# Reciprocal of the denominators by ln and exp on ScalarE, four more matmuls of zeros, and a newly searched order of the units

## The chip, the cores and the metric

The kernel runs on one core of a Trainium2 chip. The metric is the device time of one execution in microseconds (us), as the median of several runs; lower is better. The five engines of the core work side by side, each through its own list of instructions in order: PE (TensorE, with its weight loads PEld), DVE (VectorE), ACT (ScalarE), POOL (GpSimd) and SP (SyncE), which issues all the transfers of this kernel. They wait for one another by semaphores.

## The reference

Two independent blocks share one output of 2048 x 1152. Block A is a gated long convolution over the sequence, computed in the reference with a transform of length 4096. Block B is linear attention with 32 heads of width 18.

```python
def _A_ref(q, k, v, shift_k, ssm_k, ssm_D):        # all of S=2048 by D=576
    ...
    kv = k_shift * v                               # k_shift: causal conv of k with 4 taps
    ...
    y = irfft2(rfft2(kv_pad) * rfft2(kf_pad))[:, 0, :S, :]
    y = y + kv * ssm_D[None, None, :]
    return q * y

def _B_ref(x, wqkv, wo):
    ...
    phi = lambda t: jnp.where(t > 0, t + 1, jnp.exp(t)) + 1e-6
    pq, pk = phi(q), phi(k)
    kv = jnp.einsum("bhsd,bhse->bhde", pk, v)
    z = jnp.einsum("bhsd->bhd", pk)
    num = jnp.einsum("bhqd,bhde->bhqe", pq, kv)
    den = jnp.einsum("bhqd,bhd->bhq", pq, z)[..., None] + 1e-6
    o = num / den
    return o.transpose(0, 2, 1, 3).reshape(B, S, D) @ wo
```

## The kernel before, in words

**The units.** The program is cut into some 300 units of work, each a call of a small function, and the string `ORDER` (L32 to L59) lists them in the order in which they are recorded. A unit such as `h1.0.1.0.A/12` has a name, indices, letters for the engines that do its elementwise work (A for ACT, D for DVE, P for POOL, N for leaving a step to the matmuls that follow), and after the slash the slots of PSUM and of the rings in SBUF that its tiles take. The loop at L853 to L858 calls them one after the other; the order of instructions on every engine follows from this list, and no scheduler changes it. A unit that stands late in the list waits on its engine for those ahead of it.

**Block A.** The 576 channels go in five chunks (`ci` 0 to 4). For each chunk, `cv` (L473) makes the 4-tap convolution of k and multiplies it by v, on DVE or POOL, in products of 128 x 2048 (128 x 1024 for the half chunk 4). `h1` and `u1` (`s1`, L523) multiply the filter and that product with a table of sines, 8 matmuls a unit, and copy the PSUM tile to `Ch` or `Cu`; `ht` and `ut` (`tr`, L536) turn them by a DMA transpose; `h2` and `u2` (`s2`, L544) are a second, small transform whose results are copied to `T` and `SU`; `pX`, `pT` (L565 to L569) multiply these on DVE or POOL, and `pS`, `pA` (L570 to L574) add two halves of a product. Where `pS` or `pA` is N, the unit does nothing and each `i1` of that half issues 8 matmuls more. `i1` (L576, copied to `V`) and `i2` (L595, whose result DVE multiplies by q, L604) transform back, and `st` stores. The sines themselves are made at the start: `ix` on DVE makes index tables `mp` and `mc`, `sin` on ACT (L222) turns them into `G`. Filter chunks are turned by matmuls at first (`hT`, L502); `hd` (L500) adds D to one column of the filter before that, and needs `Dcol` from `dc` (L426).

**Block B.** `xd` turns x (matmuls with the identity, or a DMA transpose), `k` (L446), `q` (L455) and `qt` (L464) project and apply phi with one Exp on ACT (L443) and one operation on DVE (L444). `G`, `zs` and `kv` make the head matrices without projecting v; `M` folds them into wo. `den` (L716) makes all denominators by 40 matmuls into a PSUM tile of 128 x 512; DVE adds an epsilon (L732, L734) and takes the reciprocal (L736) into `rden`. Four units `bc` (L738) and one `bt` (L748) spread the reciprocals over the channels by matmuls with `esel`, and DVE multiplies pq by them (L746, L755). The eight row pairs of `o` and `ol` (L757, L785) are the last matmul, copied to `ob` and stored.

**The start.** `wu` (`_warm`, L74) multiplies zeros with zeros, five matmuls of 128 x 512, before any data is there. `Wj` (L380) spreads the taps by five matmuls, whose source row `ls` loads by DMA (L373). `sw` (L225) makes the last sines and then calls an Exp of one column, so that the table of Exp is loaded early; the load shows as ACT_TABLE_LOAD.

Of the kernel before, what the change touches and what calls it, by code (L numbers as in the profile page):

```python
# [12 lines left out]
ACT = mybir.ActivationFunctionType  # L13
ALU = mybir.AluOpType
# [3 lines left out]
D = 576  # L18
# [55 lines left out]
def _warm(tc, psum, K, n):  # L74

    nc = tc.nc
    zero = K.sm[:, 1984:2048].bitcast(BF)
    ps = psum.tile([128, 4, 128], FP32, name="warm_ps")
    for _ in range({'A': 5, 'B': 8, 'C': 7, 'D': 6}[n]):
        nc.tensor.matmul(ps[:], lhsT=zero, rhs=zero.unsqueeze(1).to_broadcast([128, 4, 128]), start=True, stop=True)  # L80
# [144 lines left out]
def _sine16(tc, K):  # L225
    nc = tc.nc
# [17 lines left out]
def kernel(  # L244
# [13 lines left out]
    nc = tc.nc  # L258
# [358 lines left out]
    B = {}  # L617
# [271 lines left out]
```

## Time and profile before

| what | value |
|---|---|
| median of 3 runs | 161.67 us |
| the three runs | 161.38, 161.67, 163.29 us |
| profiled execution, first to last instruction (span) | 159.3 us |
| busy PE / DVE / ACT / POOL in the span | 147.6 / 139.8 / 128.4 / 65.2 us |
| granted TensorE clock | 1.000 |

The profiled execution has no time of its own beside its span; the median of the runs is 2.37 us above the span and the fastest run 2.08 us. In the rows of the profile the first number of a timeline is the start in us after the span's start, the second the stretch in us from the first start to the last end of the merged instructions; then come engine, line, operation, output and inputs with shapes, and the count. A row of a group ends with the total busy us and the mean ns of one. Instructions of one engine overlap a little, so a stretch of several is shorter than their durations added; matmuls overlap a great deal, and how fast they stream is read from the starts of successive rows.

### The profile page before, as it was taken

How to read it: one execution, taken by the hardware profiler on the slowest of the kernel's cores; microseconds unless marked ns; L12 is line 12 of the kernel's file. 1: busy time of each engine (PE TensorE's matmuls, PEld its weight loads, DVE VectorE, ACT ScalarE, POOL GpSimd, SP SyncE). 2: the span in 40 equal slices, each digit the busy share in tenths (PEclk: the TensorE clock that was granted, in tenths of full speed). 3: DMA queues.
4: the chain of work that ended last, by engine and by line, in shares of the span. 5: the costliest groups of instructions: out<-in, count | busy, mean ns of one | idle time of the engine just before them, and what ended most of it. 6: DMA issues, size and time to landing. Idle time of an engine off the chain costs nothing.

```text
span 159.3 us, 4563 instructions
## 1 busy us (share of the span) xinstructions
PE 147.6 (93%) x1966; PEld 92.2 (58%) x1982; DVE 139.8 (88%) x170; ACT 128.4 (81%) x157; POOL 65.2 (41%) x67
## 2 busy tenths in 40 slices
PE   6799999999999999999998999999878999998990
PEld 1498564465734467467466568576445565677550
DVE  7978699899899999999899989998999999998420
ACT  7979996899997999959996956997999685786331
POOL 7407541806510970008100019589997077400000
PEclk9999999999999999999999999999999999999999
DMA  3999999990979999999999999684999999444282
GB/s 105 352 368 294 255 239 305 152 231 3 164 130 228 243 228 240 189 212 312 159 196 272 242 155 212 187 141 90 268 152 184 175 324 204 124 117 136 62 264 100
DMA packets 74171, 31.92 MB, mean 200 GB/s; under 512 B 52074, under 2 KB 73509, under 8 KB 74150
## 3 DMA queue, kind: packets, MB, share of 16 engines
q1 hardware_dynamic: 74150, 31.62, 91.7%
q8 instruction: 15, 0.25, 0.7%
q14 instruction: 6, 0.05, 0.1%
HBM read 14.97 MB, written 4.72 MB: 124 GB/s over the span
## 4 chain that ended last, share of the span: by engine, by line
PE 66%; POOL 12%; DVE 8%; DMA 6%; issue 3%; ACT 3%; SPq 0%; DVEq 0%; ACTq 0%; POOLq 0%
PE k_ps L451 12%; PE q_ps L460 11%; PE g_ps L659 6%; PE o_ps L776 6%; PE s_ps L532 6%; POOL X L567 5%; PE s_ps L555 5%; DMA Cth<-Ch 4%; PE i_ps L589 3%; POOL T L569 3%; PE hT_ps L511 2%; DMA pqT<-in_A_shift_k_dram 2%; PE xT_ps L337 2%; PE i_ps L602 2%; PE qt_ps L468 2%
## 5 line engine op out<-in xcount | busy, mean ns | idle before, releaser
L451 PE MATMUL k_ps<-wqk,xT 128*128 128x512 bf16 (+1 forms) x154 | 21.3, 282 | 0.3
L532 PEld LDWEIGHTS <-G 128*128 128x128 bf16 x320 | 17.4, 98 | 3.7 <-issue 3.4
L299 ACT ACTIVATE Cu<-s_ps 128x1024 bf16<-128x1024 f32 (+1 forms) x18 | 16.9, 978 | 2.1 <-DMA Cth<-Ch 1.4
L460 PE MATMUL q_ps<-xT,wqk 128*128 128x512 bf16 x78 | 18.2, 379 | 0.1
L451 PEld LDWEIGHTS <-xT 128*128 128x128 bf16 x160 | 11.4, 98 | 10.5 <-issue 0.5
L299 ACT ACTIVATE Ch<-s_ps 128x1024 bf16<-128x1024 f32 (+1 forms) x17 | 15.0, 928 | 3.0 <-PE s_ps L532 2.7
L299 ACT ACTIVATE ob<-o_ps 128x576 bf16<-128x576 f32 (+1 forms) x12 | 7.5, 636 | 11.3 <-PE o_ps L768 5.1
L299 ACT ACTIVATE V<-i_ps 128x1024 bf16<-128x1024 f32 x16 | 15.7, 1034 | 1.0 <-PE i_ps L589 1.0
L659 PE MATMUL g_ps<-pk,x_sb 128*128 128x65 bf16 (+1 forms) x124 | 16.3, 283 | 0.2
L299 ACT ACTIVATE T<-s_ps 128x1024 bf16<-128x1024 f32 x16 | 15.7, 1027 | 0.5 <-POOL at L490 0.5
L490 DVE TENSOR_TENSOR at<-at 128x2048 bf16<-128x2048 bf16 (+1 forms) x13 | 14.9, 1143 | 0.7 <-POOL at L489 0.3
L489 DVE TENSOR_TENSOR at<-k,Wj 128x2048 bf16<-128x2048 bf16 (+1 forms) x13 | 14.8, 1136 | 0.4 <-POOL at L490 0.4
L776 PE MATMUL o_ps<-wo_M,pqT 128*128 128x64 bf16 (+1 forms) x108 | 13.8, 283 | 0.5 <-issue 0.5
L444 DVE SCALAR_TENSOR_TENSOR pk<-pk,k_ps 128x576 bf16<-128x576 bf16 x16 | 11.8, 751 | 2.7 <-ACT pk L443 2.6
L299 ACT ACTIVATE SU<-s_ps 128x1024 bf16<-128x1024 f32 x14 | 14.1, 1029 | 0.0
L659 PEld LDWEIGHTS <-x_sb 128*128 128x128 bf16 x128 | 8.4, 97 | 8.7 <-issue 1.1
L460 PEld LDWEIGHTS <-wqk 128*128 128x128 bf16 x80 | 7.5, 98 | 9.1 <-issue 1.1
L443 ACT ACTIVATE pk<-k_ps,neg 128x576 bf16<-128x576 f32 x16 | 11.6, 745 | 1.2 <-PE k_ps L451 0.9
L604 DVE TENSOR_TENSOR q<-i_ps,q 128x1024 bf16<-128x1024 f32 (+1 forms) x10 | 11.0, 1107 | 1.2 <-PE i_ps L603 1.2
L776 PEld LDWEIGHTS <-pqT 128*128 128x128 bf16 x112 | 7.4, 98 | 7.6 <-issue 0.9
L490 POOL TENSOR_TENSOR at<-at 128x2048 bf16<-128x2048 bf16 (+1 forms) x2 | 6.2, 3097 | 12.9 <-DVE at L489 12.9
L532 PE MATMUL s_ps<-v,G 128*128 128x128 bf16 (+1 forms) x160 | 10.5, 214 | 1.0 <-ACT Cu L299 0.4
(161 smaller groups left out, 349.1 us busy)
## 6 DMA issues: line engine op xcount, KB each, us to landing
x_sb<-in_B_x_dram SPq DMA_DIRECT2D x4, 576.0 KB, 4.7
h_sb<-in_A_ssm_k_dram SPq DMA_DIRECT2D x4, 512.0 KB, 5.1
out_dram<-ob SPq DMA_DIRECT2D x7, 288.0 KB, 3.3
k<-in_A_k_dram SPq DMA_DIRECT2D x1, 1280.0 KB
v<-in_A_v_dram SPq DMA_DIRECT2D x1, 1280.0 KB, 8.5
q<-in_A_q_dram SPq DMA_DIRECT2D x1, 1280.0 KB
wqk<-in_B_wqkv_dram SPq DMA_DIRECT2D x2, 576.0 KB, 7.6
k<-in_A_k_dram SPq DMA_DIRECT2D x1, 1024.0 KB
```

Source lines behind the costliest of these rows:

```text
L299: nc.scalar.activation(out=out, in_=in_, func=ACT.Copy)
L443: nc.scalar.activation(out=out_ap, in_=ps_ap, func=ACT.Exp, bias=K.neg1[0:n, :])
L444: nc.vector.scalar_tensor_tensor(out=out_ap, in0=out_ap, scalar=1.0, in1=ps_ap, op0=ALU.min, op1=ALU.max)
L451: nc.tensor.matmul(ps[:, n0:n1], lhsT=xT[r // 4][:, t, rr * 128:(rr + 1) * 128], rhs=wqk[:, t, D + n0:D + n1], start=(t == 0), stop=(t == 4))
L460: nc.tensor.matmul(ps[:, j, :], lhsT=wqk[:, t, 128 * c:128 * c + 128], rhs=xT[g][:, t, :], start=(t == 0), stop=(t == 4))
L489: on[0].tensor_tensor(out=t_, in0=kk[:, 3 - stage:19 - stage], in1=wb(stage), op=ALU.mult)
L490: on[1].tensor_tensor(out=a_, in0=a_, in1=t_, op=ALU.add)
L532: nc.tensor.matmul(ps[:, bi, 0:dc], lhsT=K.G[ri][:, b, :], rhs=xf(b), start=True, stop=True)
L555: nc.tensor.matmul(ps[q:q + 32, z, :], lhsT=K.W0[64 * z:64 * z + 64, x, :], rhs=Ct[64 * z:64 * z + 64, r, :, j, :], start=True, stop=True)
L604: nc.vector.tensor_tensor(out=qs, in0=ps[:, :, 0:dc], in1=qs, op=ALU.mult)
L659: nc.tensor.matmul(ps[:, n0:n1], lhsT=x_sb[:, r, f0:f0 + fn], rhs=pk[:, r, n0:n1], start=(r == 0), stop=(r == 15))
L776: nc.tensor.matmul(pss[i][:, n0:n1], lhsT=pqT[:, c, r * 128:(r + 1) * 128], rhs=B['M'][:, c, n0:n1], start=(c == 0 and not first), stop=(c ...
```

## The change

**The reciprocal.** `b_den` no longer adds and inverts on DVE. ACT takes Ln of the PSUM tile with the epsilon as bias, in place, and then Exp with scale -1 into `rden`. `_sine16` names the table that holds both Ln and Exp for the load that it makes anyway.

**The zeros.** A second unit `wu.2.B` issues four matmuls of zeros more, right after the first five.

**The order.** The whole list `ORDER` is another one: nearly every unit stands at another place, 49 units have other engine letters, and the slots differ. It keeps all other units.

```diff
-io dl ix.0.0/0 hl.0/0 lz sin.1.0 eps ix.1.0/1 id ls ix.0.1 iw ix.1.1 xl.2 sin.0.0 wk wu.1.A/0 lw.2 dc/1 hd.0 Wj.A/230
+io ix.0.1/0 lz lw.2 wu.1.A/0 ls wu.2.B/1 sin.1.1 ix.1.1/1 sin.0.1 xl.2 id Wj.A/230 dl dc/1 ix.0.0 hl.0/0 hd.0 ix.1.0
...
@@ _warm
-    for _ in range({'A': 5, 'B': 8, 'C': 7, 'D': 6}[n]):
+    for _ in range({'A': 5, 'B': 4}[n]):
@@ _sine16
     nc.scalar.activation(out=K.sm[:, 1536:1984], in_=K.wi, func=ACT.Sin, scale=TWO_PI / 16, bias=K.negpi[:])
+    nc.scalar.preload_act_table_set("natural_log_exp_and_others")
     nc.scalar.activation(out=K.warm[:], in_=K.neg1[:], func=ACT.Exp)
@@ b_den
         den = ps[:, 0:512]
-        nc.vector.tensor_scalar(out=den, in0=den, scalar1=ez[:, 0:1], scalar2=None, op0=ALU.add)
-        with nc.allow_low_precision(reason="the reciprocal is used as bf16"):
-            nc.vector.reciprocal(out=B['rden'], in_=den)
+        nc.scalar.activation(out=den, in_=den, func=ACT.Ln, bias=ez[:, 0:1])
+        nc.scalar.activation(out=B['rden'], in_=den, func=ACT.Exp, scale=-1.0)
```

Three places show what the new order does. The first is ACT at the start of the program, from the zeroing of the tap rows (L377) on. Before:

```order
L377 ACTIVATE pqT<-sm 96x1152
L222 ACTIVATE G_103<-mp,negpi 128x1024
L222 ACTIVATE G_132<-mc,negpi 128x1024
L432 ACTIVATE Dcol<-D_ps 128x5
L500 ACTIVATE h_sb<-h_sb,Dcol 128x1
L299 ACTIVATE Wj<-W_ps 128x4x256 x2
L299 ACTIVATE Wj<-W_ps 128x4x64
L222 ACTIVATE G_132<-mc,negpi 128x1024
L222 ACTIVATE G_103<-mp,negpi 128x1024
L500 ACTIVATE h_sb<-h_sb,Dcol 128x1
L299 ACTIVATE Ch<-s_ps 128x2x32x16 x3
```

ACT at the same place in the changed program:

```order
L377 ACTIVATE pqT<-sm 96x1152
L221 ACTIVATE G_112<-mp,negpi 128x1024
L221 ACTIVATE G_117<-mc,negpi 128x1024
L299 ACTIVATE Wj<-W_ps 128x4x256 x2
L299 ACTIVATE Wj<-W_ps 128x4x64
L432 ACTIVATE Dcol<-D_ps 128x5
L500 ACTIVATE h_sb<-h_sb,Dcol 128x1
L221 ACTIVATE G_117<-mc,negpi 128x1024
L500 ACTIVATE h_sb<-h_sb,Dcol 128x1
L299 ACTIVATE xT<-xT_ps 128x512
L221 ACTIVATE G_112<-mp,negpi 128x1024
L299 ACTIVATE Ch<-s_ps 128x2x32x16 x2
```

The copies of the taps (Wj) now stand ahead of Dcol, the last table of sines stands behind a copy of xT that DVE made before, and two copies of Ch instead of three follow. On PE the nine matmuls of zeros are followed at once by those of Wj, then by the turning of x (20 matmuls) and of both filter chunks 0 and 1 (32), before the first 24 matmuls of `h1`.

The second place is DVE around the denominators, from a copy of SU (L301) to the products with the reciprocals (pqT). Before:

```order
L604 TENSOR_TENSOR q<-i_ps,q 128x8x128
L301 CAST Ch<-s_ps 128x2x32x16
L301 CAST SU<-s_ps 128x2x512
L487 TENSOR_TENSOR at<-k,Wj 128x16x64
L489 TENSOR_TENSOR at<-k,Wj 128x16x64
L490 TENSOR_TENSOR at<-at 128x16x64
L732 TENSOR_SCALAR ez<-den_ps 128x1
L734 TENSOR_SCALAR den_ps<-den_ps,ez 128x512
L736 RECIPROCAL wo_M<-den_ps 128x512
L604 TENSOR_TENSOR q<-i_ps,q 128x8x128 x2
L746 SCALAR_TENSOR_TENSOR pqT<-pqT,bc_ps 128x1024 x2
```

DVE at the same place in the changed program:

```order
L301 CAST SU<-s_ps 128x2x512
L301 CAST V<-i_ps 128x8x32x4
L301 CAST wo_M<-m_ps 128x576
L567 TENSOR_TENSOR X<-SU,T 128x2048
L572 TENSOR_TENSOR X<-X 128x2x512
L569 TENSOR_TENSOR T<-SU,T 128x2048
L604 TENSOR_TENSOR q<-i_ps,q 128x8x128
L732 TENSOR_SCALAR ez<-den_ps 128x1
L604 TENSOR_TENSOR q<-i_ps,q 128x8x128
L745 SCALAR_TENSOR_TENSOR pqT<-pqT,bc_ps 128x1024 x2
```

The add and the reciprocal are gone, three operations of the half chunk's convolution and a copy of Ch have left, and the products X and T of chunk 2, an add, and copies of V and of M have come. On ACT the Ln and the Exp stand behind a copy of SU and ahead of four copies of Cu.

The third place is POOL in the second half, behind the copy of the filter's half chunk (hp). Before:

```order
L518 COPY hp<-h_sb 64x2048
L489 TENSOR_TENSOR at<-k,Wj 128x16x64
L490 TENSOR_TENSOR at<-at 128x16x64
L567 TENSOR_TENSOR X<-SU,T 128x2048
L569 TENSOR_TENSOR T<-SU,T 128x2048
L572 TENSOR_TENSOR T<-T 128x2x512
L567 TENSOR_TENSOR X<-SU,T 128x2048
```

POOL at the same place in the changed program, where the first row of the half chunk's convolution stands ahead of that copy:

```order
L487 TENSOR_TENSOR at<-k,Wj 128x16x64
L518 COPY hp<-h_sb 64x2048
L489 TENSOR_TENSOR at<-k,Wj 128x16x64
L490 TENSOR_TENSOR at<-at 128x16x64
L567 TENSOR_TENSOR X<-SU,T 128x2048
L489 TENSOR_TENSOR at<-k,Wj 128x16x64
L490 TENSOR_TENSOR at<-at 128x16x64
L489 TENSOR_TENSOR at<-k,Wj 128x16x64
```

POOL has given its products of chunk 2 and one of chunk 3 to DVE and taken most of the convolution of the half chunk.

49 lines of the change are left out of this document (24 added, 25 removed).

## The prediction

> **What bounds the kernel now.** I read the page first (span, busy shares, slices), then a table by stage, then the two places that the change rewrites.
>
> ```profile
> span 159.3 us, 4563 instructions
> PE 147.6 (93%) x1966; PEld 92.2 (58%) x1982; DVE 139.8 (88%) x170; ACT 128.4 (81%) x157; POOL 65.2 (41%) x67
> GB/s 105 352 368 294 255 239 305 152 231 3 164 130 228 243 228 240 189 212 312 159 196 272 242 155 212 187 141 90 268 152 184 175 324 204 124 117 136 62 264 100
> ```
>
> Three engines are above 80%, so no single one is worth its busy time; the question is which ends last in each stage. The stages are cut at the first matmul of `k` (14.84), at the first product of `i2` on DVE (95.67) and at the last product with a reciprocal (122.31):
>
> ```profile
> core 0: us, PE busy (x) PEld busy (x) DVE busy (x) ACT busy (x) POOL busy (x), PEclk, DMA share, GB/s
> 0.00:14.84 14.84, 12.02 (x120) 9.02 (x120) 12.08 (x27) 12.77 (x18) 6.97 (x31) 1.00 0.89 279
> 14.84:95.67 80.83, 79.69 (x905) 45.95 (x915) 75.31 (x82) 70.81 (x83) 25.41 (x26) 1.00 1.06 209
> 95.67:122.31 26.64, 24.11 (x455) 16.61 (x454) 25.99 (x33) 23.48 (x31) 24.16 (x8) 1.00 0.90 179
> 122.31:140.00 17.69, 17.14 (x284) 10.84 (x282) 16.58 (x19) 12.91 (x17) 8.62 (x4) 1.00 0.91 202
> 140.00:159.30 19.30, 14.66 (x226) 9.82 (x222) 9.86 (x12) 8.47 (x11) 0.00 (x0) 1.00 0.45 132
> ```
>
> From 14.84 to 95.67 PE is busy 79.69 of 80.83 us: it is the bound, and little DVE work saved there would be worth anything. From 95.67 to 122.31 DVE is busy 25.99 of 26.64 us, and PE's 24.11 us overstates it, since its matmuls overlap: DVE is the bound. At the end neither is.
>
> **The start: zeros and another order (-1.1 us).** The PE rows up to the first `k`:
>
> ```profile
> 1.06 2.31 PE L80 MATMUL warm_ps<-sm 128*128 128x512 bf16 x5 [1.06 <-DVE negpi L127]
> 5.15 2.08 PE L387 MATMUL W_ps<-pqT,sm 97*128 97x512 bf16 x5 [1.56 <-DMA pqT<-in_A_shift_k_dram]
> 7.02 1.91 PE L511 MATMUL hT_ps<-ident,h_sb 128*128 128x128 bf16 x16
> 8.73 1.71 PE L337 MATMUL xT_ps<-ident,x_sb 128*128 128x128 bf16 x16
> 10.28 0.39 PE L342 MATMUL xT_ps<-ident,x_sb 128*128 128x128 bf16 x4
> 14.84 6.43 PE L451 MATMUL k_ps<-wqk,xT 128*128 128x512 bf16 x49
> ```
>
> and from the chain of waits a later group of the same width, at full pace:
>
> ```profile
> 21.27 0.89 PE s_ps L532 x16
> ```
>
> The first transposes go at (8.73 - 7.02) / 16 = 107 ns each, the later matmuls at 0.89 / 16 = 56 ns; the column of the granted clock reads 1.00 all the same. The turns of x in between take (10.28 - 8.73) = 1.55 us, 0.16 us less than sixteen at 107 ns, so the rate doubles about three matmuls before 10.28, near 10.1 us. This is 5 us after the matmuls start again at 5.15, behind a gap in which PE had nothing to do; the five zeros before the gap did not bring it about. W_ps (four matmuls of 512 columns and one of 256) takes 7.02 - 5.15 = 1.87 us, 0.42 us for 512 columns; nine zeros at that pace run from 1.06 to about 5.0. They fill the gap, cost nothing (W_ps waits for its taps until 5.15 anyway, and by the shapes the taps' transfer now has one of 144 KB ahead of it instead of one of 512 KB), and keep PE busy without a break from 1.06 on.
>
> If the 5 us of unbroken work are what counts, the rate doubles at 1.06 + 5 = 6.1; if the 9 us since the first matmul count, it stays at 10.1. I take 6.8, nearer to the first, since the row shows a gap that the zeros close. W_ps then still ends at 7.0 at the slow rate, and the turning of x and of two filter chunks (20 + 32 matmuls) takes 52 x 0.056 = 2.9 us instead of up to 5.6. What PE can use of this is set by ACT and DVE, by these rows:
>
> ```profile
> 6.20 2.22 ACT L299 ACTIVATE Wj<-W_ps 128x1024 bf16<-128x1024 f32 x3 [0.18 <-PE W_ps L387]
> 8.29 1.16 ACT L222 ACTIVATE G<-mc,negpi 128x1024 bf16<-128x1024 int16 x1
> 10.37 0.30 ACT L500 ACTIVATE h_sb<-h_sb,Dcol 128x1 bf16<-128x1 bf16 x1
> L299 ACT ACTIVATE xT<-xT_ps 128x512 bf16<-128x512 bf16 x1 | 0.6, 600 | 0.0
> L299 ACT ACTIVATE T<-s_ps 128x1024 bf16<-128x1024 f32 x16 | 15.7, 1027 | 0.5 <-POOL at L490 0.5
> ```
>
> After the change ACT goes Wj to 8.4, Dcol and the first h_sb (0.1 + 0.3) to 8.8, G to 9.9, h_sb to 10.1, xT to 10.7, the last G to 11.8. Only then can the third unit of `h1` run: 8 matmuls to 12.2, their copy with the one ahead to about 13.4, the second copy of xT (0.6) to 14.0, and `k` starts at about 14.2 instead of 14.84, with five units of `h1` behind it instead of four (8 x 0.056 = 0.45 us). Gain 0.64 + 0.45 = 1.1 us. Bounds: with the rate doubling at 4.5, Wj and all behind it come 0.5 us sooner: -1.6. With the rate doubling at 10.1 as now, the turns end some 1.7 us later, DVE copies the second filter chunk until about 13.4, and `k` starts near 15.6: +0.3.
>
> The Trainium skill, page "TensorE: Matmul & The Clock Gate", section "Part 1: The HAM clock gate (the "warmup" mystery)", has the clock double after one busy window of about 3.4 us that runs freely; an estimate from that page puts it between 4.5 and 7.9 us here, where the start would be worth -1.6 to about -0.8. Its Part 4 says that transposes do not count as busy; here the rate doubled after three microseconds of transposes alone, so the trace speaks against that. If it held, only 1.06 to 7.0 would count, and a whole window would fall in it about 7 times in 10; the rest would be the +0.3.
>
> **Sixteen fewer matmuls (-0.5 us).** The list of before has five N among `pS` and `pA`, by the extra matmuls of `i1`; the list of after has 16 matmuls of `i1` fewer. The chain of waits prices them:
>
> ```profile
> 73.56 2.34 PE i_ps L589 x80
> ```
>
> 16 x 2.34 / 80 = 0.47 us of PE's own stream, on the path wherever PE is the bound.
>
> **The denominators and DVE's middle stage (-2.0 us).** DVE before, from the copy of Ch:
>
> ```profile
> 99.34 1.20 DVE L301 CAST Ch<-s_ps 128x1024 bf16<-128x1024 f32 x1
> 101.60 0.86 DVE L487 TENSOR_TENSOR at<-k,Wj 128x1024 bf16<-128x1024 bf16 x1
> 102.38 0.68 DVE L489 TENSOR_TENSOR at<-k,Wj 128x1024 bf16<-128x1024 bf16 x1
> 103.09 0.69 DVE L490 TENSOR_TENSOR at<-at 128x1024 bf16<-128x1024 bf16 x1
> 103.96 0.76 DVE L734 TENSOR_SCALAR den_ps<-den_ps,ez 128x512 f32<-128x512 f32 x1
> 104.76 3.36 DVE L736 RECIPROCAL wo_M<-den_ps 128x512 bf16<-128x512 f32 x1
> 115.42 6.89 DVE L746 SCALAR_TENSOR_TENSOR pqT<-pqT,bc_ps 128x1024 bf16<-128x1024 bf16 x6
> ```
>
> The prices of what comes, and of what ACT pays:
>
> ```profile
> L567 DVE TENSOR_TENSOR X<-SU,T 128x2048 bf16<-128x2048 bf16 x7 | 9.0, 1285 | 0.2 <-ACT SU L299 0.2
> L569 DVE TENSOR_TENSOR T<-SU,T 128x2048 bf16<-128x2048 bf16 x7 | 8.5, 1218 | 0.4 <-POOL X L567 0.4
> L572 DVE TENSOR_TENSOR X<-X 128x1024 bf16<-128x1024 bf16 x4 | 2.7, 684 | 0.0
> L301 DVE CAST V<-i_ps 128x1024 bf16<-128x1024 f32 x2 | 2.4, 1220 | 0.0
> L301 DVE CAST ob<-o_ps 128x576 bf16<-128x576 f32 x4 | 3.0, 751 | 3.9 <-PE o_ps L768 3.9
> L443 ACT ACTIVATE pq<-qt_ps,neg 128x512 bf16<-128x512 f32 x2 | 1.4, 690 | 0.0
> L569 POOL TENSOR_TENSOR T<-SU,T 128x2048 bf16<-128x2048 bf16 x2 | 8.1, 4070 | 5.8 <-DVE X L567 5.7
> ```
>
> Out between the first `i2` and the last `bc` on DVE: 0.76 + 3.36 + (0.86 + 0.68 + 0.69) + 1.20 = 7.55 us. In: X 1.29, its add 0.68, T 1.22, V 1.22, M at ob's 0.75 = 5.16 us. Net -2.4 us. So more than half of the reciprocal's 4.1 us is spent again, on products that POOL made before at 4.07 us each. No row shows Ln, or Exp to this tile; the Exp of 128 x 512 from PSUM takes 0.69 us, so the two cost ACT 1.4 us (at worst two copies of 1024 columns, 2.1 us; never a gain). In the list they stand behind one copy of SU, and PE has 8 + 8 + 16 matmuls' work (i2 and two `u1`, about 1.8 us) between the denominators and the first `bc`: the chain 0.15 + 1.4 us and its handovers fits, just. ACT's load in this stage rises by these 1.4 us and by copies: one of Ch and one of T come (2 x 1.03), one of V and one of M go (1.03 and about 0.7, by the widths), +0.3. That makes 23.48 + 1.7 = 25.2 us against DVE's 25.99 - 2.4 = 23.6: ACT is late next. It would allow 26.64 - 25.2 = 1.4 us, and some more because its copies overlap by about 0.1 us each (two of 1.03 take 1.94 at 145.22, below). I take -2.0, nearer to DVE's -2.4. Bounds: -4.1, if the chain from the denominators to the products alone sets the end; 0, if ACT's new place in the order makes it wait.
>
> **The end (+0.5 us).** From 122.31 on DVE's work falls by some 2.7 us at the same prices, but DVE is idle 9.4 of the last 19.3 us, so I cost that at nothing. The new list puts `i2` of the half chunk right behind the second `i1` of that chunk; before, an `i2` of another chunk stood between, and even so:
>
> ```profile
> 145.22 1.94 ACT L299 ACTIVATE V<-i_ps 128x1024 bf16<-128x1024 f32 x2 [0.80 <-PE i_ps L589]
> PE i_ps L602 <- ACT V L299: 0.6, 1, 0.6
> ```
>
> PE waited 0.6 us for those two copies; without the 0.9 us of cover it waits up to 1.5. Two thirds of it may return, since `o` behind it finds ACT less crowded: +0.5, bounds 0 and +1.
>
> **The sum.** -1.1 - 0.5 - 2.0 + 0.5 = -3.1 us against the profiled span of 159.3: 156.2. The median of the runs stands 2.37 us above that span, so 161.67 - 3.1 = 158.6 us. About 2% (3.2 us) is what a measurement of this kernel tells from no change: the likeliest case lies just inside it.
>
> **The rivals.**
> The whole chain counts. If PE waits in the middle stage only through the reciprocal, the full 4.1 us go and the end costs nothing: -1.1 - 0.5 - 4.1 = -5.7, 156.0 us. For it: the six products at 115.42 run without a gap to 122.31, and `o` waits for them. Against it: DVE got 5.2 us of other work there.
> No help from clock or DVE. The rate still doubles at 10.1 (+0.3), ACT takes all that DVE gives (0), the end costs +1: with the -0.5 that is +0.8, 162.5 us. For it: ACT would stand at 25.2 of 26.6 us.
> A transpose comes late (the other side). The first turn of Ch is needed earlier: the page of before has it at
>
> ```profile
> 14.54 5.75 SPq L539 DMA_TRANSPOSE Cth<-Ch x1
> 31.02 0.56 PE s_ps L555 x16
> ```
>
> 16.5 us ahead of its matmuls. In the new order six `k` (7.4 us by the rows at 14.84), two units of `h1` (0.9) and a `q` (2.2) stand between, so PE wants it at about 24.7, while DVE finishes the last quarter of Ch behind a copy of xT, near 17.4. With 5.75 us it lands at 23.2, 1.5 us early. Some 8 us more would be needed to end over 2% slower than before (1.5 + 3.1 + 3.2): a queue blocked by the loads that stand beside it (1.0 MB of v, 0.6 MB of x at the 239 to 305 GB/s of those slices are 5 to 7 us). Then 165 us or more.
> That the Ln brings a third table load is excluded by the list: it has two, as before.
>
> **How the numbers follow.** Likeliest case (157.4 to 160.2) 0.47, of which a third lies below 158.4, the 2% line; whole chain 0.26; no help 0.18; late transpose 0.09. Faster by over 2%: 0.26 + 0.16 = 0.42. Within 2%: 0.31 + 0.18 = 0.49. Slower: 0.09. The range reaches from the whole chain to no help, 155.8 to 162.6, and leaves out the late transpose (0.09) and about a third of the whole chain's cases, which lie lower (0.09).
>
> **What would show it.** The start is right if the transposes of the changed kernel go at 56 ns from about 7 us and `k` starts near 14.2; wrong if they go at 107 ns to 10. The middle is right if Ln and Exp take 0.6 to 0.8 us each, and the stretch from the first `i2` product to the last `bc` product shrinks from 26.6 to about 24.6 with ACT as busy as DVE; if it shrinks to 22.5 the whole chain counted. The end is right if PE waits 1 to 1.5 us for V behind the last `i1`. A wait of PE for a DMA of Cth near 25 us would show the late transpose.

## The result: slower by 4.0%, and the profile after

| what | before | after |
|---|---|---|
| median of 4 runs each | 161.70 us | 167.94 us |
| the runs | 161.38 to 163.29 us | 166.70 to 168.56 us |
| ratio to before, 95% interval | | 1.0398 [1.0339, 1.0457] |
| span of the profiled execution | 159.3 us | 166.9 us |
| granted TensorE clock, mean | 1.000 | 0.988 |
| busy PE / DVE / ACT / POOL | 147.6 / 139.8 / 128.4 / 65.2 us | 149.2 / 141.7 / 131.6 / 74.0 us |

The forecast was 158.6 us, in a range of 155.8 to 162.6. The kernel is slower, and the range does not hold the time. The ratios, here and below, leave out a kernel's runs that lie over 1.5% above its fastest.

The table by stage of the kernel after, cut at the same three events (first matmul of `k`, first product of `i2` on DVE, last product with a reciprocal); the columns are the stretch, the busy time of PE, PEld, DVE, ACT and POOL, the granted clock, the DMA share and GB/s:

```profile
0.00:14.86 14.86, 12.51 (x132) 8.69 (x133) 12.09 (x25) 12.75 (x18) 6.76 (x30) 1.00 0.85 262
14.86:95.37 80.51, 79.50 (x890) 45.18 (x900) 75.60 (x82) 71.24 (x86) 34.01 (x29) 1.00 1.02 215
95.37:127.73 32.36, 24.58 (x433) 16.70 (x433) 30.02 (x33) 23.55 (x29) 26.93 (x10) 0.95 0.71 135
127.73:166.90 39.17, 32.62 (x513) 20.93 (x512) 23.95 (x28) 24.02 (x31) 6.33 (x3) 0.99 0.66 163
```

Against before the stages are 0.02 us longer, 0.32 shorter, 5.72 longer (32.36 against 26.64) and 2.18 longer (39.17 against 36.99), which makes the 7.6 us of the spans. So three quarters of the loss lie in the middle stage, the one that the prediction expected to gain 2.0 us.

The timeline of DVE there in the kernel after (start, length, engine, line, operation):

```profile
102.89 3.66 DVE L567 TENSOR_TENSOR X<-SU,T 128x2048 bf16<-128x2048 bf16 x1
106.58 2.50 DVE L572 TENSOR_TENSOR X<-X 128x1024 bf16<-128x1024 bf16 x1
109.00 3.13 DVE L569 TENSOR_TENSOR T<-SU,T 128x2048 bf16<-128x2048 bf16 x1
112.06 1.21 DVE L604 TENSOR_TENSOR q<-i_ps,q 128x1024 bf16<-128x1024 f32 x1
113.19 0.14 DVE L732 TENSOR_SCALAR ez<-den_ps 128x1 f32<-128x1 f32 x1
```

and POOL's at the same time:

```profile
101.54 3.92 POOL L518 COPY hp<-h_sb 64x2048 bf16<-64x2048 bf16 x1
105.42 3.11 POOL L489 TENSOR_TENSOR at<-k,Wj 128x1024 bf16<-128x1024 bf16 x1
108.61 2.44 POOL L490 TENSOR_TENSOR at<-at 128x1024 bf16<-128x1024 bf16 x1
111.02 5.04 POOL L567 TENSOR_TENSOR X<-SU,T 128x2048 bf16<-128x2048 bf16 x1
```

Read the two side by side. X, its add and T were priced at 1.29, 0.68 and 1.22 us; they read 3.66, 2.50 and 3.13, 6.1 us more. X is issued at 102.89 while POOL copies until 105.46, and ends 1.1 us after that: nearly its own length. POOL's next product begins at 105.42 and ends at 108.53, 2.0 us after X is done, about the 2.1 us that it takes alone; and so on in turn, each one ending when its own work has followed the end of the other engine's. The product `q` at 112.06 reads PSUM and takes its usual 1.21 us, although POOL is in a product of 5 us.

What waits behind that: `ez` and so the Ln on ACT,

```profile
113.43 0.66 ACT L734 ACTIVATE den_ps<-den_ps,ez 128x512 f32<-128x512 f32 x1 [4.62 <-DVE ez L732]
114.12 0.60 ACT L735 ACTIVATE wo_M<-den_ps 128x512 bf16<-128x512 f32 x1
```

and PE, by its table of waits (engine, tile, line, whom it waited for: total, times, longest):

```profile
PE i_ps L602 <- ACT V L299: 3.5, 2, 2.1
PE s_ps L532 <- DVE q L604: 3.0, 1, 3.0
PE D_ps L430 <- DMA sm<-in_A_ssm_D_dram: 1.2, 1, 1.2
...
PE s_ps L555 <- DMA Cth<-Ch: 0.9, 1, 0.9
```

Ln and Exp take 0.66 and 0.60 us, as forecast. ACT stands idle for 4.6 us before them: PE's last matmuls of the denominators end at 109.33, and DVE comes to `ez` 3.9 us later, at 113.19. PE waits 3.0 us for DVE to free the tile that `q` reads, and 2.1 us in the middle and 1.4 us at the end for ACT's copies of V, where 0.6 us at the end was all before.

### The profile page after: what moved, and what is told of

It reads as the page before. It is cut to its first block, busy times and chain, and to the rows that moved or that the text cites. A ratio compares the mean times of both kernels' runs of the same rounds, so it can differ in the third digit from the quotient of the medians.

```text
span 166.9 us, 4537 instructions
## 1 busy us (share of the span) xinstructions
PE 149.2 (89%) x1953; PEld 91.5 (55%) x1970; DVE 141.7 (85%) x164; ACT 131.6 (79%) x161; POOL 74.0 (44%) x70
## 4 chain that ended last, share of the span: by engine, by line
PE 45%; DVE 23%; DMA 13%; POOL 9%; ACT 5%; issue 2%; SPq 1%; DVEq 0%; POOLq 0%; ACTq 0%
PE g_ps L659 9%; DMA Ctu<-Cu 6%; PE k_ps L451 6%; PE s_ps L532 5%; PE o_ps L775 5%; PE i_ps L589 4%; DMA Cth<-Ch 3%; PE s_ps L555 3%; DMA sm<-in_A_ssm_D_dram 3%; DVE at L490 3%; DVE at L489 3%; POOL at L489 2%; POOL at L490 2%; DVE X L567 2%; PE i_ps L602 2%
## 5 line engine op out<-in xcount | busy, mean ns | idle before, releaser
L451 PE MATMUL k_ps<-wqk,xT 128*128 128x64 bf16 (+1 forms) x155 | 21.1, 283 | 0.3
L489 POOL TENSOR_TENSOR at<-k,Wj 128x1024 bf16<-128x1024 bf16 (+1 forms) x5 | 15.5, 3101 | 7.5 <-issue 7.4
L299 ACT ACTIVATE SU<-s_ps 128x1024 bf16<-128x1024 f32 x16 | 15.8, 1022 | 2.1 <-PE s_ps L555 2.1
L299 ACT ACTIVATE T<-s_ps 128x1024 bf16<-128x1024 f32 x17 | 16.8, 1019 | 0.2 <-PE s_ps L555 0.2
L299 ACT ACTIVATE Cu<-s_ps 128x1024 bf16<-128x1024 f32 (+1 forms) x16 | 15.4, 1000 | 1.4 <-DMA Cth<-Ch 0.9
L299 ACT ACTIVATE Ch<-s_ps 128x1024 bf16<-128x1024 f32 (+1 forms) x16 | 14.2, 918 | 1.9 <-PE s_ps L532 1.9
L572 POOL TENSOR_TENSOR T<-T 128x1024 bf16<-128x1024 bf16 x3 | 6.4, 2125 | 20.8 <-ACT ob L299 14.7
L490 DVE TENSOR_TENSOR at<-at 128x2048 bf16<-128x2048 bf16 (+1 forms) x12 | 14.2, 1179 | 0.8 <-POOL at L489 0.4
L299 ACT ACTIVATE ob<-o_ps 128x576 bf16<-128x576 f32 (+1 forms) x13 | 8.2, 636 | 8.0 <-PE o_ps L767 4.2
L569 DVE TENSOR_TENSOR T<-SU,T 128x2048 bf16<-128x2048 bf16 x9 | 12.9, 1433 | 0.0
```

The costliest lines, as they stand in the source:

```text
L299: nc.scalar.activation(out=out, in_=in_, func=ACT.Copy)
L451: nc.tensor.matmul(ps[:, n0:n1], lhsT=xT[r // 4][:, t, rr * 128:(rr + 1) * 128], rhs=wqk[:, t, D + n0:D + n1], start=(t == 0), stop=(t == 4))
L489: on[0].tensor_tensor(out=t_, in0=kk[:, 3 - stage:19 - stage], in1=wb(stage), op=ALU.mult)
L490: on[1].tensor_tensor(out=a_, in0=a_, in1=t_, op=ALU.add)
L569: e.tensor_tensor(out=t[:], in0=s['SU', hf][:], in1=t[:], op=ALU.mult)
```

## The experiments

Theory 1 after the result: DVE's products from SBUF and POOL's work exclude each other, and the new order puts them side by side ahead of the denominators. Theory 2: PE's waits for V, and the drop of the clock behind its waits, carry the time, and the collision only fills idle time of DVE. Theory 3: the small parts (Ln and Exp, zeros) cost it. The first four kernels take the change apart; all their ratios are to the kernel before on the same chip.

**DVE's three operations moved behind the last reciprocal product (e1).**

```diff
-u2.2.1.1.A/03 pX.2.0.D/0 pA.2.0.D cv.4.0.P pT.2.0.D
+u2.2.1.1.A/03 cv.4.0.P
...
-h1.4.0.1.A/2 bc.1/30 ut.3.1/0
+h1.4.0.1.A/2 bc.1/30 pX.2.0.D/0 pA.2.0.D pT.2.0.D ut.3.1/0
```

> The changed kernel, with X, its add and T of chunk 2 (first half) moved on DVE from ahead of the denominators to behind the last bc product, where POOL's block of work should be nearly over. Nothing is left out. Port theory (a DVE operation with two inputs in SBUF and a POOL operation shut each other out): the stretch from the first i2 product to the last bc product falls from 32.4 us to 23 to 25 us, the three operations take their 1.2, 0.7 and 1.2 us again, ACT no longer waits 4.6 us for ez, and the time is 161 to 163 us. Chain theory (the handovers DVE, ACT, ACT, PE of ln and exp hold PE): the time stays above 166 us, since the chain is the same. Transfer theory (late transposes at the end): 165 us or more, since the end keeps its 39 us.

Measured: 167.61 us, ratio 1.038 [1.0317, 1.0444], the same as the change itself. DVE's part of the timeline in this run:

```profile
106.57 1.23 DVE L604 TENSOR_TENSOR q<-i_ps,q 128x1024 bf16<-128x1024 f32 x1 [4.61 <-PE i_ps L603]
109.83 0.16 DVE L732 TENSOR_SCALAR ez<-den_ps 128x1 f32<-128x1 f32 x1 [2.04 <-PE den_ps L729]
...
123.66 1.22 DVE L567 TENSOR_TENSOR X<-SU,T 128x2048 bf16<-128x2048 bf16 x1
124.92 0.69 DVE L572 TENSOR_TENSOR X<-X 128x1024 bf16<-128x1024 bf16 x1
```

and what PE met there:

```profile
126.80 0.40 PE L589 MATMUL i_ps<-W,T 64*128 64x128 bf16 x4 [2.90 <-DVE T L569]
```

Away from POOL the operations have their old lengths, and the collision is gone. The stretch from the first `i2` product (94.39) to the last product with a reciprocal (which ends at 123.75) is 29.36 us, 3.0 us shorter, where theory 1 had expected 23 to 25; but T is now late for PE by 2.9 us, and the 2.1 us for V stay. The time of 161 to 163 us that theory 1 expected did not come: the run put a wait of the same size elsewhere, so it does not show what the collision costs as a whole.

**Add and reciprocal back on DVE and the named table left out, all else as after the change (e2).**

```diff
-        nc.scalar.activation(out=den, in_=den, func=ACT.Ln, bias=ez[:, 0:1])
-        nc.scalar.activation(out=B['rden'], in_=den, func=ACT.Exp, scale=-1.0)
+        nc.vector.tensor_scalar(out=den, in0=den, scalar1=ez[:, 0:1], scalar2=None, op0=ALU.add)
+        nc.vector.reciprocal(out=B['rden'], in_=den)
```

> The changed kernel, with the add and the reciprocal back on DVE and the table of Exp alone; order and zeros as changed. Port theory: the reciprocal reads PSUM and is not shut out, so it adds its 4.1 us to DVE behind ez less some 1.3 to 2 us of the ACT chain: 169.5 to 171.5 us. Chain theory: without the handovers to ACT 165 us or less.

Measured: 171.23 us, 1.0603 [1.055, 1.0656]. In the new order PE stands right behind the reciprocal:

```profile
116.59 0.39 PE L741 MATMUL bc_ps<-wo_M,esel 32*128 32x512 bf16 x2 [3.27 <-DVE wo_M L735]
```

Against the change itself (167.94) Ln and Exp are worth 3.3 us in the new order. So they are not what made it slower.

**Only Ln and Exp, in the kernel before (e3).** The edit is the one of `b_den` and the named table.

> The kernel before, in its own order, with only the reciprocal by ln and exp. Port theory (the reciprocal is not what went wrong): DVE is the bound from 95.7 to 122.3 us and loses 4.1 us of work while ACT gets 1.3, so 158 to 160.5 us. Chain theory: the chain on ACT is late, 162.5 us or more.

Measured: 161.97 us, 1.0014 [0.998, 1.0049], no change; neither expectation holds the time. The middle stage, cut at the same events as before (first product of `i2`, last product with a reciprocal), and what DVE does with the time it is given:

```profile
95.51:123.22 27.71, 24.29 (x455) 16.69 (x454) 22.02 (x32) 24.70 (x33) 24.48 (x8) 1.00 0.95 180
```

```profile
108.97 1.22 DVE L605 TENSOR_TENSOR q<-i_ps,q 128x1024 bf16<-128x1024 f32 x1 [5.28 <-PE i_ps L604]
```

DVE's load falls from 25.99 to 22.02 us, and DVE simply stands still for 5.28 us until PE delivers the next `i2`. The stage is even 1.07 us longer (27.71 against 26.64). The reason is on ACT, where Ln and Exp (1.3 us) now stand ahead of the copies of V that this `i2` reads. ACT before, and in this run:

```profile
104.75 1.94 ACT L299 ACTIVATE V<-i_ps 128x1024 bf16<-128x1024 f32 x2
...
105.88 1.95 ACT L300 ACTIVATE V<-i_ps 128x1024 bf16<-128x1024 f32 x2
```

PE starts that `i2` at 106.75 before and at 107.88 here, each time right behind the copies. And DVE's second product of `i2` waited for PE already before, soon after the reciprocal, which ended at 108.12:

```profile
109.61 1.23 DVE L604 TENSOR_TENSOR q<-i_ps,q 128x1024 bf16<-128x1024 f32 x1 [0.42 <-PE i_ps L603]
```

DVE was full, and was not the bound.

**Only the four zeros, in the kernel before (e4):** `wu.2.B/1` behind `wu.1.A/0`.

> The kernel before, in its own order, with only the four more matmuls of zeros behind the first five. If unbroken work doubles PE's rate earlier: transposes at 56 ns from about 7 us, the first k at 13.6 to 14.4 us instead of 14.84, and a time of 160.6 to 161.4 us. If the start is held by ACT, DVE and the transfers anyway: the first k at 14.7 to 14.9 us and 161.5 to 161.9 us.

Measured: 160.66 us, 0.9946 [0.9912, 0.998]: 0.9 us faster. PE at the start of this run:

```profile
5.31 1.13 PE L387 MATMUL W_ps<-pqT,sm 97*128 97x512 bf16 x5
6.28 1.15 PE L511 MATMUL hT_ps<-ident,h_sb 128*128 128x128 bf16 x16
7.27 1.06 PE L337 MATMUL xT_ps<-ident,x_sb 128*128 128x128 bf16 x16
...
13.61 2.56 PE L451 MATMUL k_ps<-wqk,xT 128*128 128x512 bf16 x17
```

W_ps ends 0.97 us after its start (6.28 - 5.31) where it took 1.87, and sixteen transposes take (7.27 - 6.28) = 0.99 us, 62 ns each: the rate has doubled at 5.31 already in this execution, and `k` starts at 13.61 instead of 14.84.

**Both small parts in the kernel before (e5).**

> The kernel before in its own order, with both small parts of the change: Ln and Exp on ACT, and four more matmuls of zeros. The ln and exp alone left the time as it was and the zeros alone gained 0.9 us. If DVE's stage is covered by PE (theory now), the two add up to the zeros alone: 160.4 to 161.0. If the earlier start had made DVE the bound of the middle stage, so that the freed 4.1 us count now: 158.5 to 160.0. The new order is the only part that is left out, so a time below the kernel before puts all of the loss on the order.

Measured: 160.36 us, 0.9926 [0.9886, 0.9966]. The two add up to the zeros alone, as far as the intervals tell. This is the fastest version of the study, 0.7% below the kernel before; what is left out of it is the new order, so the loss is in the order.

**The exclusion by itself (m1).** The kernel leaves the whole computation out and writes zeros; it runs products of 2048 columns on DVE and POOL, alone and side by side.

> Leaves the whole computation out (it writes zeros) and only runs DVE and GpSimd operations of this kernel's shapes, first alone, then side by side. Theory 1 (the two engines exclude one another whenever DVE reads two operands from SBUF, for the whole of an instruction): the 2048-wide product takes 1.2 us on DVE and 4.1 us on POOL alone; side by side the two alternate, so that a DVE product reads 4 to 5 us while POOL works and POOL's reads 5.3, and the sum of both lists is the time. Beside a DVE product that reads PSUM both keep their times (1.2 us per 1024 columns, 4.1 us). A DVE copy of 2048 from SBUF to SBUF could go either way. Rival (the long products in the trace of the changed kernel come from something else, such as a shared bank or the transfers): DVE 1.2 to 1.5 and POOL 4.1 to 4.5 in every pairing.

Its timeline (start, stretch, operation, count). Alone, then DVE's products from SBUF, DVE's products of 1024 columns from PSUM, and DVE's copies within SBUF, each beside six products of POOL:

```profile
18.43 7.52 DVE L37 TENSOR_TENSOR dc<-da,db 128x2048 bf16<-128x2048 bf16 x6
...
26.96 16.41 POOL L49 TENSOR_TENSOR pc<-pa,pb 128x2048 bf16<-128x2048 bf16 x4
...
43.61 37.57 DVE L37 TENSOR_TENSOR dc<-da,db 128x2048 bf16<-128x2048 bf16 x12
...
44.84 28.97 POOL L49 TENSOR_TENSOR pc<-pa,pb 128x2048 bf16<-128x2048 bf16 x6
...
81.74 15.06 DVE L41 TENSOR_TENSOR dc<-pq,da 128x1024 bf16<-128x1024 f32 x12
...
82.04 24.70 POOL L49 TENSOR_TENSOR pc<-pa,pb 128x2048 bf16<-128x2048 bf16 x6
...
106.97 31.18 DVE L45 COPY dc<-da 128x2048 bf16<-128x2048 bf16 x12
...
107.66 26.30 POOL L49 TENSOR_TENSOR pc<-pa,pb 128x2048 bf16<-128x2048 bf16 x6
```

Alone a product takes 7.52 / 6 = 1.25 us on DVE and 16.41 / 4 = 4.10 on POOL. Both lists one after the other would be 12 x 1.25 + 6 x 4.10 = 39.6 us; side by side they take 37.57. So 2.0 us of 39.6 overlap. Products that read PSUM keep 15.06 / 12 = 1.25 us and leave POOL at 24.70 / 6 = 4.12. What one DVE operation takes while POOL works, from the groups within POOL's stretch (count, then busy and mean ns), for products and for copies within SBUF:

```profile
L37 DVE TENSOR_TENSOR dc<-da,db 128x2048 bf16<-128x2048 bf16 x6 | 29.8, 4974 | 0.2
...
L45 DVE COPY dc<-da 128x2048 bf16<-128x2048 bf16 x6 | 26.6, 4441 | 0.2
```

A product takes 5.0 us instead of 1.25. A copy is shut out likewise: 4.4 us, where the last five, after POOL is done, take 0.69 each. POOL's copies beside DVE's products, a fourth pairing, stretch them too (12 products in 24.60 us instead of 15.0). Theory 1's mechanism holds, and the rival to it falls.

**POOL out of the way (e6).** In the changed kernel, the conv of the half chunk goes to DVE for its first two steps, and POOL's copy `hp` is made earlier; DVE's X, add and T stay where they are.

```diff
-pA.1.0.P M.2.D/1 ... pA.2.0.D cv.4.0.P pT.2.0.D i1.1.0.0.A/0 ... u1.3.0.1.A/02 hT.4.p/01 ... cv.4.1.PP
+pA.1.0.P hT.4.p/01 M.2.D/1 ... pA.2.0.D pT.2.0.D cv.4.0.D i1.1.0.0.A/0 ... u1.3.0.1.A/02 ... cv.4.1.DD
```

> The changed kernel with POOL out of the way of DVE's products of chunk 2: the first two steps of the half chunk's convolution (three products of 1024 columns) go to DVE, and POOL's copy of the filter's half chunk is done earlier. DVE keeps X, the add and T where they are. Theory 1 (the collision of DVE and POOL on SBUF costs the time): X, the add and T take 1.3 to 1.8, 0.7 and 1.2 us, ez runs near 109.5 instead of 113.2, PE's wait of 3.0 us for q is gone, and the stretch from the first i2 product to the last bc product is 28 to 29.5 us instead of 32.4; the time falls by 3 to 4 us, to 163.5 to 165. Theory 2 (PE's waits for the copies V and the clock that falls behind them cost it, and the collision only fills DVE's idle time): the times of X and T fall, PE still waits 3.5 us for V, and the time stays at 166.5 to 168.

Measured: 164.81 us, 1.0189 [1.0127, 1.0251]. The same operations on DVE:

```profile
101.92 1.65 DVE L567 TENSOR_TENSOR X<-SU,T 128x2048 bf16<-128x2048 bf16 x1
103.61 0.69 DVE L572 TENSOR_TENSOR X<-X 128x1024 bf16<-128x1024 bf16 x1
104.22 1.22 DVE L569 TENSOR_TENSOR T<-SU,T 128x2048 bf16<-128x2048 bf16 x1
...
123.42 3.12 DVE L569 TENSOR_TENSOR T<-SU,T 128x2048 bf16<-128x2048 bf16 x1
```

and the middle stage, up to the last product with a reciprocal:

```profile
94.44:123.51 29.07, 24.30 (x421) 15.81 (x421) 26.24 (x36) 23.34 (x29) 16.52 (x7) 0.96 0.78 154
```

DVE has three more operations, the stage is 3.3 us shorter (29.07 against 32.36), and the time falls by 3.1 us. Theory 1 is right as to the largest part: half of the loss. (X keeps 0.36 us of the collision, the end of `hp`. A new collision came with the edit: T of the second half, at 123.42, takes 3.12 us where it took 1.22 after the change, since POOL's part of the half chunk now stands beside it. The same holds in e7 and e15.)

**And cover for V (e7).** As e6, with `u2.2.1.0` and `den` ahead of the first `i2` of chunk 1.

```diff
-i1.1.0.1.A/1 i2.1.0/2 u2.2.1.0.A/3 den/0 i2.1.1/1
+i1.1.0.1.A/1 u2.2.1.0.A/3 den/0 i2.1.0/2 i2.1.1/1
```

> As the run with POOL out of the way, and PE's u2 unit and the matmuls of the denominators stand ahead of the first i2 of chunk 1, so that PE has 2 us of work while ACT copies V. Theory 1: the collision was nearly all, so this brings at most 1 us more than the run with POOL out of the way alone. Theory 2: PE's wait for V at this place falls from 2.1 to under 1 us, the clock stays near 1.0 in the stage, the stage takes 26.5 to 27.5 us, and the time is 161 to 163.5, at least 1.5 us below the run without the cover.

Measured: 163.95 us, 1.0143 [1.0071, 1.0215]: 0.9 us less than e6, which ran beside it. PE's wait of 2.1 us became 0.5. The gain is inside theory 1's number (at most 1 us) and short of theory 2's (at least 1.5); the clock did not stay up:

```profile
119.21 0.41 PE L555 MATMUL s_ps<-Cth,W 64*32 64x512 bf16 x8 [1.21 <-DVE pqT L745]
...
121.00:122.00 1.00, 0.95 (x20) 0.34 (x16) 1.00 (x2) 0.90 (x3) 1.00 (x1) 0.57 1.13 216
122.00:123.00 1.00, 1.00 (x24) 0.76 (x18) 1.00 (x2) 1.00 (x2) 0.92 (x2) 0.50 1.18 214
123.00:124.00 1.00, 1.00 (x24) 1.00 (x21) 1.00 (x1) 0.89 (x1) 1.00 (x1) 0.50 0.75 150
124.00:125.00 1.00, 1.00 (x21) 0.78 (x16) 1.00 (x1) 0.11 (x1) 0.61 (x1) 0.72 1.19 123
```

The first row is PE's wait of 1.2 us, which ended at 119.21. In the other rows, of 1 us each, the granted clock is halved for about 3.4 us, some 2 us after that wait.

**A failed edit: the half chunk's convolution behind `bc` (e8), and two more on top of it.** `cv.4.1.DD` goes behind `bc.1`, and the copy of T at `h2.3.0.0` to ACT.

> As the run with cover for V, and the two products of the half chunk's convolution that stood between DVE's products with the reciprocals go behind them, and the copy of T there goes to ACT. Theory now (the rest of the middle stage's loss is PE waiting for DVE to free a PSUM tile of bc, 1.2 us, and a drop of the granted clock to 0.66 for 5 us that follows): the last bc product ends near 120 instead of 122.7, PE's wait of 1.2 us for pqT goes, and if the clock stays at 1.00 too, the time falls by 1 to 2.5 us to 161.5 to 163; if the clock drops all the same, by 0.5 to 1. Rival (POOL, now late with the half chunk, or the DMA transposes are what the end waits for): same time as before this edit, 163.7 to 164.2, with the wait moved to Cu or Cth of the half chunk.

Measured: 172.01 us, 1.0721 [1.0676, 1.0767]. Its PE meets the rival:

```profile
133.02 1.04 PE L532 MATMUL s_ps<-v,G 128*128 128x64 bf16 x16 [7.34 <-DVE v L493]
```

The chain of the half chunk's convolution over DVE and POOL had no room left (PE waits 0.4 us for this v in e7), and 5.7 us of delay (its product L489 on DVE at 122.28 instead of 116.62) came back as 7.3 us of wait. e9 is e8 with one `i2` of chunk 3 as cover between the second `i1` of the half chunk and its first `i2` (`i2.3.0/2` behind `i1.4.0.1.A/0`):

> As the run with the convolution behind bc, and one i2 of chunk 3 moved between the second i1 of the half chunk and its first i2, as it stood before the change. The prediction's step on the end: PE's wait of 1.4 us for V becomes 0.4 to 0.6, and the time falls by 0.5 to 0.9 us. If o behind it gives it back: by less than 0.3.

Measured: 170.85 us, 1.0639 [1.058, 1.0697], 1.16 us less than e8 beside it, though the intervals of the two overlap; PE's wait of 1.4 us for V fell to 0.4. e10 is e9 with the transfer of D first (`dl` behind `lz`):

> As the run with cover at the end, and the transfer of D (1 KB) is issued first, as before the change, instead of behind three larger ones. PE no longer waits at D_ps (1.2 us in the profiled run of the changed kernel, 0.0 to 0.6 in the others), k starts at 13.7 to 13.8. If the wait occurs in most runs: 0.3 to 1.0 us faster; if it was rare: within 0.2 us of the run before it. All steps undone, the new order should stand level with the kernel before, 160.0 to 162.

Measured: 170.83 us, 1.0642 [1.059, 1.0694], the same as e9. Its wait at D_ps is gone, but in its profile W_ps ran at the slow rate (1.94 us) and `k` started at 14.07, so in this kernel, where PE later stands 5.8 us before v of the half chunk, the order of this transfer is worth nothing that can be told. Whether it is worth something in a kernel without that wait was not tried.

**The half chunk on POOL beside products from PSUM (e11), with cover at the end (e12).** e11 is e7 with `cv.4.1.PP` and `h2.3.0.0.A/0`, so that POOL works while DVE's products read PSUM. e12 adds the move of `i2.3.0`.

> As the run with cover for V, but the second step of the half chunk's convolution (two products) goes back to POOL, where it now stands beside DVE's products with the reciprocals, which read PSUM and share nothing with POOL; the copy of T there goes to ACT. So DVE's products run without the 2.6 us between them and the half chunk's convolution ends earlier, not later. Theory now (what is left of the middle stage's loss is DVE's other work between its products with the reciprocals, and the half chunk must not come later): last bc product near 120 to 120.5 instead of 122.7, no wait of PE for v over 0.5 us, 162 to 163.2 us. Rival (those 2.6 us were covered by PE's own work and copies by ACT, as the reciprocal was in the order before): the products end earlier, PE waits elsewhere, and the time stays at 163.7 to 164.2.

> As the run with the half chunk on POOL, and one i2 of chunk 3 between the second i1 of the half chunk and its first i2. In the run where the half chunk came late this gave 1.2 us. Theory: PE's wait of 1.4 us for V falls to 0.4 and the time by 0.5 to 1.2 us, so that the new order with its steps undone ends at 161 to 162.3, level with the kernel before or up to 0.5 us slower. Rival: the end is set by the stores behind o and not by PE; less than 0.3 us.

Measured: e11 164.91 us, 1.017 [1.0114, 1.0226]; e12 164.40 us, 1.0127 [1.0066, 1.0189]. Both lie above what their theories expected (162 to 163.2 and 161 to 162.3 us). e11 gained nothing: DVE's products with the reciprocals now wait 1.2 and 1.8 us for PE's `bc`, so the 2.6 us between them had been covered, and POOL's conv came so early that it met the add of X. The collision at T of the second half is gone (1.22 us again), and this one stands in its place, as e12's DVE shows:

```profile
103.73 2.50 DVE L572 TENSOR_TENSOR X<-X 128x1024 bf16<-128x1024 bf16 x1
```

e12 says how much the clock takes: its two runs at a granted clock of 1.000 took 162.70 and 162.97 us, its three at 0.979 took 164.59 to 164.94, nearly 2 us more. A mean of 0.979 over 161 us is, as an estimate, 0.021 x 161 / 0.5 = 6.8 us at half clock, two stretches of 3.4 us. That the clock makes the whole of the 2 us is read from the times going with it; no run sets the clock by itself.

**The last collision removed (e14), and the cover at the end alone on e7 (e15).** e14 is e12 with POOL's product X of chunk 2 ahead of `cv.4.1.PP`.

> As the run with cover at the end and the half chunk on POOL, but POOL does its product X of chunk 2 before those two steps of the convolution, so that none of them runs beside DVE's add of 1024 columns, which took 2.50 us there instead of 0.69. Theory (the exclusion of DVE and POOL still holds a part of what is left): the add takes 0.7 us, q and the Ln come 0.8 us earlier, PE's wait of 1.1 us for q shrinks to 0.4 or less, and the time falls by 0.5 to 1.2 us, to a ratio of 1.005 to 1.010. Rival (the rest is not in that wait): ratio 1.011 to 1.015 as before.

> As the run with cover for V in the middle (conv of the half chunk's second step on DVE), with the cover at the end added and nothing else. Theory: PE's wait of 1.4 us for V at the end falls to 0.4 and the time by 0.5 to 1.2 us against 163.95, to a ratio of 1.007 to 1.011. Rival (the stores at the end set it): ratio 1.013 to 1.016.

Measured: e14 has 163.47 us and a ratio of 1.0091 [1.006, 1.0122], against 1.0127 for e12: its add takes 0.69 us again, PE's wait for q fell from 1.1 to 0.4 us, and the ratio is where the theory had it (1.005 to 1.010). A gain in time is not shown all the same. The two intervals overlap, and the ratios do not count alike: e12's holds its three runs at a clock of 0.979, e14's leaves out its two (165.27 and 165.59 us). The medians of all runs give e14 163.47 / 161.38 = 1.013, which is e12's ratio; at a clock of 1.000 e14 took 162.20 us and e12 162.70 and 162.97. e15, at 163.98 us, has 1.0137 [1.0109, 1.0165] against 1.0143 for e7: the cover at the end bought nothing there that can be told, though PE's wait did fall to 0.4 us. With e9 (1.16 us) and e12 (0.5) beside it, the price of that wait stays open between 0 and 1.2 us.

## Why the prediction was wrong, point by point

**The denominators and DVE's middle stage (-2.0 us; measured +5.7): the step that failed.** Two errors are in it.

The first is the sentence "DVE is the bound", read from a busy share of 25.99 of 26.64 us. e3 takes 4.0 us off DVE in that order and the time stays (1.0014): DVE was full because it had work that nobody waited for. What it went by was PE's `i2`, and that went by ACT's copies of V, which Ln and Exp made 1.1 us later; the prediction's lower bound, 0 if ACT's new place in the order makes it wait, was the case there. A busy share says that an engine has no room, not that the others wait for it. In the order before there was next to nothing to gain: behind the reciprocal DVE had to wait for PE's next `i2` anyway (0.42 us at 109.61). The question "who waits for this operation?" was to be put to PE's waits, which show 0.2 us for `q` and none for the reciprocal. In the new order PE does stand behind it, and there Ln and Exp are worth 3.3 us (e2).

The second is the price of what comes in. X, the add and T were taken at 3.2 us from group means of the order before. There POOL's long block of work, from 103.92 to 122.65, stands beside DVE operations that all read PSUM (the add, the reciprocal, the products `q` and pqT, a copy of T), so the groups held hardly any collision. In the new order POOL is busy 10.00 of the 10 us from 95 to 105 and 9.92 of the next 10, and they took 9.3. The bounds reached from -4.1 to 0 and held no such case. The profile of before had a sign of it, a group mean (1285 ns for X) that hides one product of 1.68 us at 133.93 beside POOL, which I did not ask about. The Trainium skill states the rule, on its page "SBUF — State Buffer", section "SBUF: two separate sides": DVE and GpSimd share one port pair, which is locked for a whole instruction, against a DVE operation with two inputs from SBUF. The runs agree (5.0 us instead of 1.25 beside POOL in m1, 1.25 from PSUM); it was the rule that spoke against this change, and I did not weigh it.

The sizes, by the runs: keeping the two engines apart gave 3.1 us back (e6), cover for V in the middle 0.9 (e7), and for the last collision no gain is shown (e14 against e12). With all of it undone e14 stands at 1.0091, or at 1.013 with all its runs. A part of that may be the halved clock: e14's one run at a clock of 1.000 took 162.20 us, the runs of before at 1.000 beside it 161.31 to 162.00. The kernel before took 161.02 to 161.75 at a clock of 0.989, so nothing is seen there of what such a stretch costs. Another part may be the start: PE waits for D in most of the profiled executions of the new order, 1.16 us in the change itself, 0.58 in e6, 1.92 in e14. No run took D's transfer by itself in this kernel, so what the rest is made of stays open.

**The start (-1.1).** The mechanism is right and the size nearly so: the zeros alone start `k` 1.2 us earlier and give 0.9 us (e4). When the rate doubles is another matter: by 5.31 in e4, where I took 6.8, but with the same nine zeros it differs from one execution to the next. W_ps is fast from 4.31 on in e1 (its row has 1.14 us) and slow to about 6.8 in e10 and e11 (1.94 and 1.98). In the profiled execution of after nothing of it is left, because the new order issues the transfer of D behind three larger ones and PE waits for it:

```profile
7.70 0.27 PE L430 MATMUL D_ps<-sm 1*128 1x1 bf16 x5 [1.16 <-DMA sm<-in_A_ssm_D_dram]
7.91 1.07 PE L337 MATMUL xT_ps<-ident,x_sb 128*128 128x128 bf16 x16
...
14.86 1.31 PE L451 MATMUL k_ps<-wqk,xT 128*128 128x512 bf16 x5
```

I counted the transfers ahead of the taps and not those ahead of D. In e6 and e7, with the same start, `k` began at 13.92 and 13.71.

**Sixteen fewer matmuls (-0.5).** The second stage is 0.32 us shorter; no run took this part alone, so its size is not shown.

**The end (+0.5; measured +2.2).** The sign and the wait are right: PE waits 1.42 us for V, forecast 1 to 1.5. The size is not: on top come 0.94 us for a transpose of Cth of the half chunk, which lands later, and a mean clock of 0.99 over 39 us, 0.4 us by an estimate (0.01 x 39).

**The rivals.** No rival was the one that happened, though what "no help" said of ACT came about in the old order (e3). The late transpose was the only one on the slower side, and PE has no wait for Cth near 25 us; the slower side deserved a case for POOL, since the list of the change itself shows products of chunk 2 moving to DVE beside a POOL with more work.

## What to carry to other kernels

Before an elementwise operation is moved to DVE, lay POOL's timeline beside its new place: a DVE product or copy that reads only SBUF costs its own time plus what is left of POOL's operation, and one that reads PSUM does not; so give POOL its work beside DVE's evictions from PSUM, as the order before did (that this pays in time e11 did not show). A full engine is the bound only where someone's wait names it; take its work away in one run before costing a change by its busy share. When a chain is moved, ask how much room its last reader had (here 0.4 us).

## What the runs showed of the hardware

DVE's copies within SBUF are shut out by POOL as its products are (in m1 4.4 us each of 2048 columns while POOL works, 0.69 alone), and POOL's own operations grow as well (2.1 to 3.1 us, 4.1 to 5.0).

The granted clock halves for about 3.4 us at a time, in some executions for twice that (e11, from 119.2 to 126), and here after short waits: in e7 PE's longest wait in the 20 us ahead of it was 1.2 us. The mean clock of one kernel differs from run to run (e12: 162.7 and 163.0 us at a clock of 1.000, 164.2 at 0.989, 164.6 to 164.9 at 0.979), which fits none, one or two such stretches. The Trainium skill, page "TensorE: Matmul & The Clock Gate", section "Part 1: The HAM clock gate (the "warmup" mystery)", has the clock fall after an idle window of about 3.4 us; the length of the stretches agrees with such a window, the waits of 1.2 us ahead of it do not. In the kernel after the change PE waited longer ahead of such a stretch, 3.0 us up to 113.32. Which pattern of waits sets it off was not tried.

Ln and Exp of 128 x 512 from PSUM take 0.66 and 0.60 us on ACT, against 0.76 and 3.36 us for the add and the reciprocal on DVE.
